# Relative-position attention and a gated MLP on one core: both heads' scores side by side in 64-row tiles, in three products

## Chip, cores, metric

The kernel runs on one core of a Trainium2 chip. The metric is the device time of one execution in microseconds, as the median of several. The engines of the core are PE (matrix products and transposes), DVE, ACT and POOL (element-wise work), and SP, which issues most transfers. PEld in a row of the profile is PE's weight load, which runs beside its matmuls.

## What is computed

```python
scores = (q @ k.T) / sqrt(64)               # batch 8, heads 8, 576 positions, 64 wide
x = log1p(|i - j|) / log1p(max(i, 1))
scores += (relu(x * w1 + b1) @ w2)          # a bias for each head and pair (i, j)
attn = softmax(scores);  y = attn @ v       # y: 4608 tokens x 512
out = ((y @ moe_w1) * (y @ moe_w2)) @ moe_w3 @ moe_w_out
```

All arrays are float32. To keep their precision at the speed of PE's rounded float32 (fp32r), a factor x is split into a rounded part h and the rest l = x - h, and the product is made as a sum of products of such parts.

## The kernel before

**Prologue.** The bias of every head is built with matmuls (L517, tile `bacc`), scaled by ACT (L530, `bev`) and written to memory (`nb_d`). From there it is loaded for each pair of heads as `nb0`, `nb1`, `nb4`, `nb5` and `nbM`.

**Attention.** A unit is one pair of heads of one batch, `units = [(p, b) ...]`: 4 pairs x 8 batches = 32 units. The 576 queries of a head are four tiles of 128 and 64 left over. Tile t = 0 to 7 is head t % 2, queries (t // 2) x 128 on; tile M holds the last 64 queries of both heads in its two halves of partitions. A unit goes through these steps:

- `ldk`, `ldq`, `ldv`: SP loads q, k, v. On the host, q and k were laid out transposed with each head twice, 64 rows above and the same 64 rows below (`_np.concatenate([a, a], axis=2)`), 1152 columns for the two heads.
- `gk`, `gq` (`op_g`): POOL rounds k into K and makes kl = k - K. In Q the upper 64 rows are the rounded part of q and the lower 64 are its rest, so that one product over 128 rows adds both parts.
- `S0` to `S7`, `SM` (`op_S`, L290): PE makes the scores of a tile into `s`, which is two PSUM banks (576 columns as 2 x 288). A tile takes four matmuls, Q with K and with kl for each half of the columns. The pool `ps_s` has two such buffers.
- `T0` to `TM` (`op_T`, L298): DVE adds the bias, scales, and takes the row maximum: `ts`, `mx`. `ts` has three buffers.
- `E0` to `EM` (`op_E`, L321): ACT makes the exponential into `pp` (or `ppM`) and the row sum into `sum`.
- `F0` to `F7`, `FM`, `L0`, `L1`, `N` (`op_F`): PE transposes 128 x 128 blocks into `pst`, four of them in a PSUM bank; `ps_t` has four buffers. N transposes the last columns of tile M and the reciprocals `r`.
- `H...` (`op_H`): ACT or DVE copies `pst` into `pt` and `px`; the table below says which.
- `r`, `rd` (`op_r`): DVE makes the reciprocals of a unit's nine columns of sums (L328, L329); after N and HN they are stored to `r_d` by two transfers.
- `W0`, `W1` (`op_W`, L397): PE multiplies by v, in two tiles of 64 columns of the array at once. `X0`, `X1` copy the result, and `xd` stores it.
- `c0` to `c7`: a piece of the MoE weights is loaded and converted in 24 of the units; c3 to c6 are on DVE.

The order on each engine is written out by hand: `ORDER` gives each step a time within a unit, the next unit's steps follow `PERIOD = 15.82` later, and `drive` issues all steps sorted by time. So an engine runs its instructions in the order of this table, steps of two units mixed, and a step that has to wait holds up what is behind it on its engine:

```python
    "PE": {
        "S0": 0.00, "S1": 1.66, "S2": 2.64, "S3": 4.31, "S4": 5.18, "S5": 8.31, "S6": 8.84, "F0": 9.37, "F1": 12.87,
        "S7": 13.32, "F4": 13.86, "SM": 14.31, "F5": 15.37, "L0": 16.35, "F2": 16.58, "F7": 17.03, "F3": 18.01,
        "FM": 18.99, "L1": 19.44, "F6": 19.67, "N": 20.66, "W0": 21.63, "W1": 25.74,
    },
```

**MoE.** Behind attention the inner weights w3 and w_out are multiplied together (`fold`, L619), and then for each chunk of 512 tokens come `up` (L661) and `down` (L686), three products each. `load_x` reads the attention's result and the reciprocals (`xr`, `rb`), and `split_x` multiplies them.

Of the kernel before, what the change touches and what calls it, by code (L numbers as in the profile page):

```python
# [31 lines left out]
PERIOD = 15.82  # L32
ORDER = {
# [5 lines left out]
    "DVE": {
        "T0": 0.98, "T1": 2.64, "T2": 3.63, "T3": 5.29, "T4": 6.16, "c3": 7.31, "c4": 8.31, "T6": 9.82, "T5": 10.52,  # L40
        "c5": 11.22, "c6": 12.22, "T7": 14.31, "H4": 15.01, "TM": 15.82, "HL0": 17.50, "r": 17.84, "HM": 20.14,
        "HN": 22.68,
    },
# [23 lines left out]
def relpos_attention_moe(  # L67
# [132 lines left out]
    for i in range(2):
        qt = qk.tile([P, 2 * (S + P)], F32R, name=f"Q{i}")
        nc.gpsimd.memset(f(qt[:, S:S + P]), 0.0)
        Q2.append(qt)

    def halves(x):
        return x.rearrange("p (a j) -> p a j", a=2)
# [38 lines left out]
    def op_g(u, n):  # L248

        d = st[u]  # L250
        x = d.pop("r" + n)
        if n == "q":
            Q = Q2[u % 2]
            Qd = halves(Q)[:, :, 0:S]
            x = halves(x)
# [1 line left out]
            nc.gpsimd.tensor_tensor(Qd[hi], x[hi], f(Qd[hi]), op=ALU.subtract)
            d["Q"] = Q
        else:
            K = qk.tile([P, 2 * S], F32R, name="K", bufs=2)  # L260
            kl = qk.tile([P, 2 * S], F32R, name="kl", bufs=2)
            nc.gpsimd.tensor_scalar(K, x, 1.0, 1.0, op0=ALU.mult, op1=ALU.mult)
            nc.gpsimd.tensor_tensor(kl, x, f(K), op=ALU.subtract)
            d.update(K=K, kl=kl)

    def op_S(u, t):
        d = st[u]
        Q, K, kl = d["Q"], d["K"], d["kl"]
        d["s", t] = ps_s.tile([P, 2, 512], F32, name="s")
        for hf in range(2):  # L270
            scores(d["s", t][:, hf, :HS], t, hf, Q, K, kl)

    def scores(s, t, hf, Q, K, kl):
        js = slice(hf * HS, (hf + 1) * HS)
        if t == "M":

            l, m = Q[:, 512:512 + P], Q[:, S + 64:S + 64 + P]
            ops = [(s, l, x[:, js]) for x in (K, kl)]
            if hf == 0:
                ops += [(s, m, x[:, S + 64:S + 64 + HS]) for x in (K, kl)]  # L280
            else:
                ops += [(s[:, 0:512 - HS], m, x[:, S + 64 + HS:2 * S]) for x in (K, kl)]
                ops += [(s[:, 512 - HS:HS], m, x[:, S:S + 64]) for x in (K, kl)]
        else:
            h, i = int(t) % 2, int(t) // 2
            q0 = h * (S + P + 64) + i * P
            l = Q[:, q0:q0 + P]
            ops = [(s, l, x[:, h * S + hf * HS:h * S + (hf + 1) * HS]) for x in (K, kl)]
        for m, (o, l, r) in enumerate(ops):
            nc.tensor.matmul(o, l, r, start=(m == 0), stop=(m == len(ops) - 1))  # L290
# [17 lines left out]
    def op_E(u, t):  # L308
        d = st[u]
        ts, mx = d.pop(("t", t))  # L310
        if "sum" not in d:
# [9 lines left out]
        nc.scalar.activation(pp, ts, AF.Exp, bias=mx, scale=-1.0, accum_out=d["sum"][:, col:col + 1])  # L321

    def op_r(u, n):
        p, b = units[u]
        d = st[u]
        if n == "":
            r = sm.tile([P, 9], F32, name="r")
            nc.vector.tensor_scalar(r, d["sum"], 1e-9, None, op0=ALU.add)  # L328
            nc.vector.reciprocal(r, r)  # L329
            d["r"] = r  # L330
        else:
            rows = r_d[p][:, b * S:(b + 1) * S]
            nc.sync.dma_start(rows[:, 0:512].rearrange("h (i j) -> h i j", j=P), d["rt"][0:8])
            nc.sync.dma_start(rows[:, 512:S].rearrange("(o h) j -> o h j", o=1), d["rt"][8:9])

    def op_F(u, n):
# [1 line left out]
        ps = ps_t.tile([P, 512], F32, name="pst")  # L340
        if n == "N":
            nc.tensor.transpose(ps[lo, 0:P], d["PM"][:, 512:S], ident)
            nc.tensor.transpose(ps[:, P:2 * P], d["PM"][:, S - P:S], ident)
            nc.tensor.transpose(ps[0:9, 2 * P:3 * P], d["r"], ident)
        elif n[0] == "L":
            for c in range(2):
                nc.tensor.transpose(ps[:, c * P:(c + 1) * P], d["P", 2 * int(n[1]) + c][:, 512:512 + P], ident)
        else:
            for c in range(4):
                if n == "M":  # L350
                    x = d["PM"][:, c * P:(c + 1) * P]
                else:
                    c0 = int(n) % 2 * (S + 64) + c * P
                    x = d["P", int(n) // 2][:, c0:c0 + P]
                nc.tensor.transpose(ps[:, c * P:(c + 1) * P], x, ident)  # L355
# [452 lines left out]
```

## Time and profile before

| | |
|---|---|
| device time, median of 3 runs | 1243.39 us (1242.02 to 1244.5) |
| span of the profiled execution | 1241.4 us, 2.0 us below that median |
| attention, first score matmul to last W1 matmul | 63 to 602 us |
| PE, DVE, ACT, POOL busy | 97%, 53%, 49%, 31% of the span |
| granted PE clock | 1.00 from 93 us on |
| DMA | 130.25 MB in 60795 packets |

Each row of the timeline gives start, length, engine, line, operation, output <- inputs, shape and count, and in brackets the idle time ahead of it with what ended it. A matmul's row is longer than its slot, since matmuls are pipelined: its slot is the distance to the next start. PE runs attention with hardly a hole, so its share of 97% says that it is occupied, not that its array is filled.

### The profile page before, as it was taken

The numbers are of one execution on the slowest core, as the hardware profiler recorded it, in microseconds if no ns is written. First come the engines' busy times: TensorE is split into PE (matmuls) and PEld (weight loads), VectorE is DVE, ScalarE is ACT, GpSimd is POOL, SyncE is SP. The second block draws the span as 40 slices with busy tenths as digits, with TensorE's granted clock in tenths as the row PEclk, the third lists the DMA queues.
The fourth block names the chain that finished last, engine by engine and source line by source line (L and its number), as shares of the span: only waits on it lengthen the run. The fifth ranks groups of instructions, "written<-read, shape, count | busy, mean of one in ns | idle before, by whom it ended". The sixth has DMA issues, their size and how long they took to land. (4 is left out here: it accounts for less than half of the span.)

```text
span 1241.4 us, 19015 instructions
## 1 busy us (share of the span) xinstructions
PE 1200.8 (97%) x7136; PEld 956.6 (77%) x7136; DVE 656.6 (53%) x1380; ACT 603.5 (49%) x1303; POOL 390.0 (31%) x260
## 2 busy tenths in 40 slices
PE   7679999999999999999989999999999999999998
PEld 3168887777778887887768788888888888888887
DVE  8647776777677767776999532222222131313111
ACT  7558887888788877888544321212121212121211
POOL 0436664666456655661654300000000000000000
PEclk9879999999999999999999999999999999999999
DMA  7854446444645463431443220212111110200001
GB/s 215 286 172 143 144 149 204 133 142 145 220 133 152 152 219 120 148 94 54 135 132 117 68 74 29 68 34 65 38 51 51 51 51 35 68 34 1 29 7 34
DMA packets 60795, 130.25 MB, mean 105 GB/s; under 512 B 8992, under 2 KB 18592, under 8 KB 60704
## 3 DMA queue, kind: packets, MB, share of 16 engines
q1 hardware_dynamic: 59408, 127.32, 32.7%
q10 hardware_dynamic: 1296, 1.72, 0.5%
q8 instruction: 56, 0.92, 0.3%
q14 instruction: 35, 0.29, 0.1%
HBM read 99.10 MB, written 29.92 MB: 104 GB/s over the span
## 5 line engine op out<-in xcount | busy, mean ns | idle before, releaser
L298 DVE CUSTOM_DVE_ANT_0 ts<-s,nb 128x576 f32<-128x576 f32 x256 | 184.7, 749 | 148.1 <-ACT pt L363 74.1
L661 PE MATMUL up<-xh,wl 128*128 128x512 f32 x576 | 225.4, 391 | 0.1
L669 DVE TENSOR_TENSOR g<-up,a 128x512 f32<-128x512 f32 x72 | 49.7, 690 | 332.2 <-PE up L661 332.2
L661 PE MATMUL up<-xh,wh 128*128 128x512 f32 x576 | 225.3, 391 | 0.0
L661 PE MATMUL up<-xl,wh 128*128 128x512 f32 x576 | 225.3, 391 | 0.0
L290 PE MATMUL s<-K,Q 128*128 128x288 f32 (+2 forms) x672 | 206.0, 326 | 16.2 <-DVE mx L298 7.6
L321 ACT ACTIVATE pp<-ts,mx 128x576 f32<-128x576 f32 x256 | 196.7, 770 | 39.2 <-DVE mx L298 39.1
L290 PE MATMUL s<-kl,Q 128*128 128x288 f32 (+2 forms) x672 | 182.1, 295 | 0.0
L686 PE MATMUL o<-w3s,gh 128*128 128x512 f32 x576 | 177.8, 390 | 0.0
L666 ACT COPY a<-up 128x512 f32<-128x512 f32 x72 | 42.2, 586 | 247.5 <-PE up L661 247.5
L647 POOL TENSOR_SCALAR xh<-xr 128x512 fp32r<-128x512 f32 x36 | 23.9, 664 | 435.7 <-DVE xr L643 432.5
L290 PEld LDWEIGHTS s<-K,Q 128*128 128x128 f32 x672 | 128.3, 191 | 38.2 <-DVE mx L298 18.0
L355 PE MATMUL pst<-ident,pp 128*128 128x128 f32 x1024 | 152.8, 278 | 0.0
L363 ACT ACTIVATE pt<-pst 128x512 f32<-128x512 f32 x224 | 129.5, 594 | 34.2 <-PE pst L355 29.9
L397 PE MATMUL pst<-pt,rv 128*64 128x320 f32 (+1 forms) x1024 | 138.3, 412 | 0.0
L355 PEld LDWEIGHTS pst<-ident,pp 128*128 128x128 f32 x1024 | 118.8, 141 | 15.2 <-DVE wi L148 11.8
L672 ACT ACTIVATE gh<-g 128x512 fp32r<-128x512 f32 x72 | 45.5, 632 | 172.8 <-DVE g L669 172.8
L290 PEld LDWEIGHTS s<-kl,Q 128*128 128x128 f32 x672 | 129.0, 192 | 0.0
L661 PEld LDWEIGHTS up<-xh,wl 128*128 128x128 f32 x576 | 108.2, 188 | 23.9 <-DVE wl L582 0.5
L661 PEld LDWEIGHTS up<-xl,wh 128*128 128x128 f32 x576 | 108.3, 188 | 23.3
L661 PEld LDWEIGHTS up<-xh,wh 128*128 128x128 f32 x576 | 108.3, 188 | 23.2
L686 PEld LDWEIGHTS o<-w3s,gh 128*128 128x128 f32 x576 | 108.2, 188 | 22.8
(85 smaller groups left out, 1720.3 us busy)
## 6 DMA issues: line engine op xcount, KB each, us to landing
rk<-in_k_dram SPq DMA_DIRECT2D x31, 576.0 KB
rq<-in_q_dram SPq DMA_DIRECT2D x31, 576.0 KB
wi<-in_moe_w_dram SPq DMA_DIRECT2D x32, 512.0 KB
nb_d<-bev SPq DMA_DIRECT2D x36, 295.5 KB
rv<-in_v_dram SPq DMA_DIRECT2D x32, 320.0 KB
x_d<-x SPq DMA_DIRECT2D x32, 288.0 KB
xr<-x_d SPq DMA_DIRECT2D x36, 256.0 KB
rb<-r_d SPq DMA_DIRECT2D x72, 128.0 KB
```

What stands on the lines that cost most here:

```text
L290: nc.tensor.matmul(o, l, r, start=(m == 0), stop=(m == len(ops) - 1))
L298: nc.vector.tensor_tensor_reduce(out=halves(ts), in0=d.pop(("s", t))[:, :, :HS], in1=halves(NB[p, t]), op0=ALU.add, op1=ALU.min, scale=-1. ...
L321: nc.scalar.activation(pp, ts, AF.Exp, bias=mx, scale=-1.0, accum_out=d["sum"][:, col:col + 1])
L355: nc.tensor.transpose(ps[:, c * P:(c + 1) * P], x, ident)
L363: nc.scalar.activation(o, x, AF.Copy)
L397: nc.tensor.matmul(acc[rows], x[:, c0:c0 + D], m, start=(c == 0), stop=(c == 4))
L647: nc.gpsimd.tensor_scalar(xh, xr, 1.0, 1.0, op0=ALU.mult, op1=ALU.mult)
L661: nc.tensor.matmul(acc, l[:, cc], r, start=(n == 0), stop=(n == 3 * NC - 1))
L666: nc.scalar.copy(a, ps[0])
L669: nc.vector.tensor_tensor(g, ps[1], a, op=ALU.mult)
L672: nc.scalar.activation(gh, g, AF.Copy)
L686: nc.tensor.matmul(d["o", t], l[:, sl], folded[ft][r], start=(ft == 0 and n == 0), stop=(ft == NF - 1 and n == 2),)
```

## The change

Four things are changed.

1. q is split in both parts like k: `qh`, `ql`, `kh`, `kl`, with head 2p in the upper 64 rows and head 2p + 1 in the lower (576 columns for k, 640 for q, where 512 on holds the last queries of both heads with zeros in the other head's rows). A score is the sum of three products, hh, lh and hl, over 64 rows each. One step makes both heads' tiles, six matmuls for each half of the columns, taking turns between the rows 0 to 63 and 64 to 127, into two buffers of `ps_s`. `S1`, `S3`, `S5`, `S7` leave the table. SM makes its tile over all 128 rows with six matmuls in place of ten.
2. FM transposes the last queries in 64-row tiles, ten transposes into two `pst` buffers, and takes over the part that N had. HM is four copies on DVE in place of one, and HN's two small copies go. `ppM` becomes two fixed tiles `PM2` with 64 zero columns in front.
3. The sums of eight units are kept in one tile of 72 columns; `r`, N, HN and `rd` run only for the last unit of each pair of heads, `rd` then with sixteen transfers.
4. In `ORDER` the T's are spread anew and E2 and E3 change places; nbM is loaded by three transfers.

```diff
@@ ORDER
-        "S0": 0.00, "S1": 1.66, "S2": 2.64, "S3": 4.31, "S4": 5.18, "S5": 8.31, "S6": 8.84, "F0": 9.37, "F1": 12.87,
-        "S7": 13.32, "F4": 13.86, "SM": 14.31, "F5": 15.37, "L0": 16.35, "F2": 16.58, "F7": 17.03, "F3": 18.01,
+        "S0": 0.00, "S2": 2.64, "S4": 5.18, "S6": 8.84, "F0": 9.37, "F1": 12.87, "F4": 13.86, "SM": 14.31, "F5": 15.37, "L0": 16.35, "F2": 16.58, "F7": 17.03, "F3": 18.01,
...
@@ op_g
+        h = qk.tile([P, x.shape[1]], F32R, name=f"{n}h", bufs=2)
+        l = qk.tile([P, x.shape[1]], F32R, name=f"{n}l", bufs=2)
+        nc.gpsimd.tensor_scalar(h, x, 1.0, 1.0, op0=ALU.mult, op1=ALU.mult)
+        nc.gpsimd.tensor_tensor(l, x, f(h), op=ALU.subtract)
+        d[n] = (h, l)
+
+    TERMS = ((0, 0), (1, 0), (0, 1))
@@ op_S
+        i = int(t) // 2
+        ss = [ps_s.tile([P, 2, 512], F32, name="s") for _ in range(2)]
         for hf in range(2):
+            for m, (x, y) in enumerate(TERMS):
+                for s, rows in zip(ss, (lo, hi)):
+                    nc.tensor.matmul(
+                        s[:, hf, :HS], Q[x][rows, i * P:(i + 1) * P], K[y][rows, hf * HS:(hf + 1) * HS],
+                        start=(m == 0), stop=(m == 2),
+                    )
@@ op_r
+        if b < B - 1:
+            return
         if n == "":
+            nc.vector.tensor_scalar(sums[p], sums[p], 1e-9, None, op0=ALU.add)
+            nc.vector.reciprocal(sums[p], sums[p])
+        elif n == "d":
+            for c in range(B):
+                rows, x = r_d[p][:, c * S:(c + 1) * S], rts[p][9 * c:9 * c + 9]
...
@@ op_F
+        if n == "M":
+            d["FM"] = [ps_t.tile([P, 512], F32, name="pst") for _ in range(2)]
+            for c in range(5):
+                for h, (ps, rows) in enumerate(zip(d["FM"], (lo, hi))):
+                    x = PM2[u % 2][rows, c * P + 64:c * P + 64 + (64 if c == 4 else P)]
...
+                    nc.tensor.transpose(ps[0:x.shape[1], c * 64:(c + 1) * 64], x, ident[rows, rows])
@@ op_H
         elif n == "M":
-            move(on, (PT.rearrange("p c (a j) -> p c a j", a=2)[:, :, :, 512:S], ps.rearrange("p (c a j) -> p c a j", c=4, a=2)))
+            for h, (ps, rows) in enumerate(zip(d["FM"], (lo, hi))):
+                move(
+                    on, (PT[:, :, h * S + 512:h * S + S], ps[:, 0:256].rearrange("p (c j) -> p c j", c=4)),
+                    (PX[rows, 512:S], ps[rows, 256:320]),
+                )
```

Where it moves instructions, first on PE, from the F's ahead of the second half of a unit's scores up to W0 (`s` are score buffers, `pst` transposes, `ppM` tile M; the numbers tell buffers apart). Before:

```order
L347 MATMUL pst_2573<-ident_60,pp_2460 128x128
L355 MATMUL pst_2581<-ident_60,pp_2460 128x128 x4
L290 MATMUL s_2587<-K_2297,Q0_119 128x288
L290 MATMUL s_2587<-kl_2298,Q0_119 128x288
L290 MATMUL s_2587<-K_2297,Q0_119 128x288
L290 MATMUL s_2587<-kl_2298,Q0_119 128x288
L342 MATMUL pst_2595<-ident_60,ppM_2528 64x128
L343 MATMUL pst_2595<-ident_60,ppM_2528 128x128
L344 MATMUL pst_2595<-ident_60,r_2547 9x128
L290 MATMUL s_2599<-K_2297,Q0_119 128x288
```

At the same place on PE after:

```order
L338 MATMUL pst_1299<-ident_60,ppM1_857 64x64
L338 MATMUL pst_1300<-ident_60,ppM1_857 128x64
L343 MATMUL pst_1313<-ident_60,pp_1193 128x128
L343 MATMUL pst_1313<-ident_60,pp_1198 128x128
L347 MATMUL pst_1321<-ident_60,pp_1198 128x128 x4
L272 MATMUL s_1339<-kh_1024,qh_1105 128x288
L272 MATMUL s_1340<-kh_1024,qh_1105 128x288
L272 MATMUL s_1339<-kh_1024,ql_1106 128x288
L272 MATMUL s_1340<-kh_1024,ql_1106 128x288
L272 MATMUL s_1339<-kl_1025,qh_1105 128x288
```

S4 stands here now, twelve matmuls that alternate between two score buffers, and behind it comes W0; before, single tiles stood there, with N between them, which now runs once in eight units.

On DVE, from the T of tile 0 on (`ts` <- `s`, with the read of its maximum `mx` as a row of its own; `px` is HL0, `pt` is HM). Before:

```order
L298 ISA ts_3824,mx_3825<-s_3801,nb0_2360 128x576
L298 ISA mx_3825 128x1
L361 COPY px1_860<-pst_3814 128x256
L328 TENSOR_SCALAR r_3841<-sum_3647 128x9
L329 RECIPROCAL r_3841<-r_3841 128x9
L298 ISA ts_3855,mx_3856<-s_3835,nb1_2390 128x576
L298 ISA mx_3856 128x1
L298 ISA ts_3870,mx_3871<-s_3850,nb0_2360 128x576
L298 ISA mx_3871 128x1
L361 COPY pt1_859<-pst_3859 128x8x64
L298 ISA ts_3899,mx_3900<-s_3881,nb1_2390 128x576
```

On DVE after, from the same T to that of tile 3:

```order
L284 ISA ts_3990,mx_3991<-s_3959,nb0_2446 128x576
L284 ISA mx_3991 128x1
L353 COPY px1_863<-pst_3981 128x256
L284 ISA ts_4002,mx_4003<-s_3960,nb1_2467 128x576
L284 ISA mx_4003 128x1
L284 ISA ts_4043,mx_4044<-s_4011,nb0_2446 128x576
L284 ISA mx_4044 128x1
L353 COPY pt1_862<-pst_4026 128x4x64
L353 COPY px1_863<-pst_4026 64x64
L353 COPY pt1_862<-pst_4027 128x4x64
L353 COPY px1_863<-pst_4027 64x64
L284 ISA ts_4062,mx_4063<-s_4012,nb1_2467 128x576
```

The two rows of r are gone from this place, HL0 stands between the T's of one pair as before, and HM between the T's of the next is four copies.

More of the change, by code (lines that the diff above doesn't have):

```diff
@@ L39 @@
     "DVE": {
[L40 to L41 removed]
+        "T0": 0.90, "T1": 1.80, "T2": 3.63, "T3": 4.50, "T4": 6.16, "T5": 7.20, "c3": 8.00, "c4": 9.00, "T6": 9.90,
+        "T7": 10.80, "c5": 11.60, "c6": 12.40, "H4": 15.01, "TM": 15.82, "HL0": 17.50, "r": 17.84, "HM": 20.14,
         "HN": 22.68,
@@ L85, in relpos_attention_moe @@
     nc = tc.nc
-    NPAIR, B, _, S2 = q.shape
-    S, D, H = S2 // 2, P // 2, 2 * NPAIR
+    NPAIR, B, _, S = k.shape
+    D, H = P // 2, 2 * NPAIR
+    SP = q.shape[3]
     HID = w1.shape[1]
@@ L195, in relpos_attention_moe @@
     lo, hi = slice(0, 64), slice(64, 128)
-    NB = {}
+    NB, sums, rts = {}, {}, {}
     st = {u: {"P": [None] * 9} for u in range(NU)}
[L202 to L206, printed above, removed]
     def halves(x):
@@ L238, in load @@
         else:
-            t = raw.tile([P, 2 * S], F32, name=f"r{which}")
+            t = raw.tile([P, src.shape[3]], F32, name=f"r{which}")
         queue = nc.scalar if u == 0 and which != "v" else nc.sync
@@ L266, in op_S @@
+        l = qk.tile([P, x.shape[1]], F32R, name=f"{n}l", bufs=2)
[3 more added lines that the diff above has]
+    TERMS = ((0, 0), (1, 0), (0, 1))
     def op_S(u, t):
         d = st[u]
-        Q, K, kl = d["Q"], d["K"], d["kl"]
-        d["s", t] = ps_s.tile([P, 2, 512], F32, name="s")
-        for hf in range(2):
[L271 to L290, printed above, removed]
@@ new lines, in op_S @@
+        Q, K = d["q"], d["k"]
+        if t == "M":
+            s = d["s", t] = ps_s.tile([P, 2, 512], F32, name="s")
+            for hf in range(2):
+                for m, (x, y) in enumerate(TERMS):
+                    nc.tensor.matmul(
+                        s[:, hf, :HS], Q[x][:, 512:512 + P], K[y][:, hf * HS:(hf + 1) * HS], start=(m == 0), stop=(m == 2),
+                    )
+            return
+        i = int(t) // 2
+        ss = [ps_s.tile([P, 2, 512], F32, name="s") for _ in range(2)]
@@ L292, in op_T @@
+        for hf in range(2):
+            for m, (x, y) in enumerate(TERMS):
+                for s, rows in zip(ss, (lo, hi)):
+                    nc.tensor.matmul(
+                        s[:, hf, :HS], Q[x][rows, i * P:(i + 1) * P], K[y][rows, hf * HS:(hf + 1) * HS],
+                        start=(m == 0), stop=(m == 2),
+                    )
+        d["s", t], d["s", str(int(t) + 1)] = ss
     def op_T(u, t):
@@ L310, in op_E @@
         ts, mx = d.pop(("t", t))
-        if "sum" not in d:
-            d["sum"] = sm.tile([P, 9], F32, name="sum", bufs=3)
+        p, b = units[u]
+        if p not in sums:
+            sums[p] = sm.tile([P, 9 * B], F32, name="sum", bufs=2)
         if t == "M":
-            pp, col = ppool.tile([P, S], F32, name="ppM", bufs=2), 8
-            d["PM"] = pp
+            pp, col = PM2[u % 2][:, P - 64:P - 64 + S], 8
         else:
@@ L320, in op_E @@
             pp, col = d["P", i][:, h * S:(h + 1) * S], i + 4 * h
-        nc.scalar.activation(pp, ts, AF.Exp, bias=mx, scale=-1.0, accum_out=d["sum"][:, col:col + 1])
+        nc.scalar.activation(pp, ts, AF.Exp, bias=mx, scale=-1.0, accum_out=sums[p][:, 9 * b + col:9 * b + col + 1])
     def op_r(u, n):
         p, b = units[u]
-        d = st[u]
+        if b < B - 1:
+            return
         if n == "":
[L327 to L334, printed above, removed]
+            nc.vector.tensor_scalar(sums[p], sums[p], 1e-9, None, op0=ALU.add)
[3 more added lines that the diff above has]
+                rows, x = r_d[p][:, c * S:(c + 1) * S], rts[p][9 * c:9 * c + 9]
+                nc.sync.dma_start(rows[:, 0:512].rearrange("h (i j) -> h i j", j=P), x[0:8])
+                nc.sync.dma_start(rows[:, 512:S].rearrange("(o h) j -> o h j", o=1), x[8:9])
@@ L338, in op_F @@
     def op_F(u, n):
         d = st[u]
-        ps = ps_t.tile([P, 512], F32, name="pst")
[L341 to L345, printed above, removed]
+        p, b = units[u]
+        if n == "N":
+            if b == B - 1:
+                ps = d["FN"] = ps_t.tile([P, 512], F32, name="pst")
+                nc.tensor.transpose(ps[0:9 * B, 0:P], sums[p], ident)
+            return
@@ new lines, in op_F @@
+        if n == "M":
[3 more added lines that the diff above has]
+                    x = PM2[u % 2][rows, c * P + 64:c * P + 64 + (64 if c == 4 else P)]
+                    if h == 1:
+                        x = PM2[u % 2][rows, 0:P] if c == 4 else PM2[u % 2][rows, (c + 1) * P:(c + 2) * P]
+                    nc.tensor.transpose(ps[0:x.shape[1], c * 64:(c + 1) * 64], x, ident[rows, rows])
+            return
@@ L346, in op_F @@
+        ps = ps_t.tile([P, 512], F32, name="pst")
+        if n[0] == "L":
             for c in range(2):
@@ L349, in op_F @@
             for c in range(4):
[L350 to L355, printed above, removed]
+                c0 = int(n) % 2 * (S + 64) + c * P
+                nc.tensor.transpose(ps[:, c * P:(c + 1) * P], d["P", int(n) // 2][:, c0:c0 + P], ident)
         d["F" + n] = ps
@@ L366, in op_H @@
         d = st[u]
+        p, b = units[u]
+        PT, PX = PTX[u % 2]
+        if n == "N":
+            if b == B - 1:
+                rts[p] = sm.tile([9 * B, P], F32, name="rt", bufs=1)
+                move(on, (rts[p], d["FN"][0:9 * B, 0:P]))
+            return
         ps = d["F" + n]
-        PT, PX = PTX[u % 2]
         if n[0] == "L":
@@ L549, in relpos_attention_moe @@
     ps_t = att.enter_context(tc.tile_pool(name="ps_t", bufs=NPS, space=PSUM))
+    PM2 = [ppool.tile([P, P - 64 + S], F32, name=f"ppM{i}") for i in range(2)]
+    for x in PM2:
+        nc.gpsimd.memset(x[:, 0:P - 64], 0.0)
     PTX = [(pt.tile([P, 4, 2 * S], F32, name=f"pt{i}"), pt.tile([P, S], F32, name=f"px{i}")) for i in range(2)]
@@ L774 @@
         a = inputs[n].reshape(-1, pairs, 2, seq, dim)
-        a = _np.stack([a[:, :, 0], _np.roll(a[:, :, 1], seq - 512, axis=2)], axis=2).transpose(1, 0, 4, 2, 3)
-        inputs[n] = _np.concatenate([a, a], axis=2).reshape(pairs, -1, 2 * dim, 2 * seq)
+        x = _np.zeros((pairs, a.shape[0], 2, dim, 640 if n == "q" else seq), a.dtype)
+        a = a.transpose(1, 0, 2, 4, 3)
+        if n == "q":
+            x[:, :, 0, :, :seq] = a[:, :, 0]
+            x[:, :, 1, :, :512], x[:, :, 1, :, seq:] = a[:, :, 1, :, :512], a[:, :, 1, :, 512:]
+        else:
+            x[:, :, 0], x[:, :, 1] = a[:, :, 0], _np.roll(a[:, :, 1], seq - 512, axis=3)
+        inputs[n] = x.reshape(pairs, -1, 2 * dim, x.shape[4])
     a = inputs["v"].reshape(-1, pairs, 2, seq, dim).transpose(1, 0, 2, 3, 4)
```

23 lines of the change are left out of this document (3 added, 20 removed), and 2 rows, old and new, of the table ORDER.

## Prediction

> **What bounds the kernel now.** I read the page first, then the busy times of single units, the waits, and last the timeline of one unit with all engines.
>
> ```profile
> span 1241.4 us, 19015 instructions
> PE 1200.8 (97%) x7136; PEld 956.6 (77%) x7136; DVE 656.6 (53%) x1380; ACT 603.5 (49%) x1303; POOL 390.0 (31%) x260
> 219.91:235.94 16.03, 15.91 (x127) 12.86 (x125) 12.20 (x31) 13.04 (x31) 10.15 (x7) 1.00 0.48 145
> PEld s L290 <- DVE mx L298: 10.6, 28, 0.5
> ```
>
> The third line is one unit of attention, from the last transpose of its N step (L344) to that of the next unit: 16.03 us, in which PE is busy for 15.91, DVE for 12.20 and ACT for 13.04, at a granted clock of 1.00. The fourth, from the waits between 100 and 555 us, says that the scores wait for T only 10.6 us in 28 units, 0.38 us a unit. So attention is a stream of PE work with hardly a hole, 32 units of it; the MoE behind it is PE too, and the change does not touch it. What counts is what a unit costs on PE, and whether PE still never waits.
>
> The durations come from this stretch of the timeline (start, length, engine, line):
>
> ```profile
> 220.42 0.29 PE L290 MATMUL s<-kl,Q 128*128 128x288 f32 x1
> 220.64 1.95 PE L397 MATMUL pst<-pt,rv 128*64 128x256 f32 x16
> 221.55 0.45 DVE L361 COPY px<-pst 64x64 f32<-64x64 f32 x2
> 222.03 0.28 DVE L361 COPY rt<-pst 9x128 f32<-9x128 f32 x1
> 222.95 0.19 PEld L290 LDWEIGHTS s<-K,Q 128*128 128x128 f32 x1 [0.39 <-DVE wmag L134]
> 224.10 0.60 PE L355 MATMUL pst<-ident,pp 128*128 128x128 f32 x4
> 224.41 0.76 DVE L298 CUSTOM_DVE_ANT_0 ts<-s,nb 128x576 f32<-128x576 f32 x1 [1.30 <-PE s L290]
> 225.10 0.75 DVE L298 CUSTOM_DVE_ANT_0 ts<-s,nb 128x576 f32<-128x576 f32 x1
> 227.48 0.66 PE L355 MATMUL pst<-ident,pp 128*128 128x128 f32 x4
> 227.89 0.38 PE L290 MATMUL s<-K,Q 128*128 128x288 f32 x1
> 228.10 0.29 PE L290 MATMUL s<-kl,Q 128*128 128x288 f32 x1
> 228.23 0.29 PE L290 MATMUL s<-K,Q 128*128 128x288 f32 x1
> 228.37 0.29 PE L290 MATMUL s<-kl,Q 128*128 128x288 f32 x1
> 228.50 0.60 PE L355 MATMUL pst<-ident,pp 128*128 128x128 f32 x4
> 228.81 0.76 DVE L298 CUSTOM_DVE_ANT_0 ts<-s,nb 128x576 f32<-128x576 f32 x1 [1.89 <-ACT pt L363]
> ...
> 229.84 0.19 PEld L290 LDWEIGHTS s<-K,Q 128*128 128x128 f32 x1
> 229.95 0.19 PEld L290 LDWEIGHTS s<-kl,Q 128*128 128x128 f32 x1
> ...
> 231.48 2.66 POOL L263 TENSOR_TENSOR kl<-rk,K 128x1152 fp32r<-128x1152 f32 x1
> 232.12 0.42 DVE L361 COPY px<-pst 128x256 f32<-128x256 f32 x1
> 232.45 1.72 DVE L328 TENSOR_SCALAR r<-sum 128x9 f32<-128x9 f32 x1
> 234.34 0.70 DVE L298 CUSTOM_DVE_ANT_0 ts<-s,nb 128x576 f32<-128x576 f32 x1
> 235.09 0.19 PEld L290 LDWEIGHTS s<-K,Q 128*128 128x128 f32 x1 [0.35 <-DVE mx L298]
> 235.33 0.29 PE L290 MATMUL s<-kl,Q 128*128 128x288 f32 x1
> ```
>
> Read off: a score matmul of 288 columns takes a slot of 0.13 us (228.10, 228.23, 228.37); after a wait the first costs 0.11 more, for its weights (235.09 to 235.33 is 0.24), and two weight loads of 128 columns with little between them stand 0.11 apart (229.84, 229.95). T starts 0.44 after the last score matmul starts (228.37, 228.81). Two T's in a row stand 0.69 apart (224.41, 225.10), and PE gets the score buffer back 0.75 after a T starts (234.34, 235.09). A transpose is a slot of 0.11 (the four of 228.50). W0 takes 2.53 from the last score matmul ahead of it to the next score weights (220.42, 222.95). F0 to F1 with W1 between takes 3.38 (224.10, 227.48), an F and the first score matmul 0.41 (227.48, 227.89). On DVE a copy of 128x256 holds its successor 0.33 (232.12, 232.45), two of 64x64 0.48 (221.55, 222.03).
>
> **The change on PE, as work.** The two heads' tiles go as 64-row halves of the array. If both halves run side by side, a pair of tiles costs six slots instead of eight: 4 pairs x 2 x 0.13 = 1.05 us less a unit. The M tile goes from six matmuls of 288 columns, two of 224 and two of 64, eight slots' worth, to six: 0.26 less. The last queries: seven transposes (four FM, three N) become ten in 64-row halves, five slots if side by side: 0.2 less, or 0.3 more if one after the other. No row shows 64-row halves; the nearest are column tiles, which do run side by side, their weights too:
>
> ```profile
> 56.24 1.06 PE L517 MATMUL bacc<-zact,w2b 128*32 128x512 f32 x1
> 56.25 1.06 PE L517 MATMUL bacc<-zdve,w2b 128*32 128x512 f32 x1
> ...
> 13.20 0.11 PEld L517 LDWEIGHTS bacc<-zact,w2b 128*32 128x32 f32 x1
> 13.21 0.12 PEld L517 LDWEIGHTS bacc<-zdve,w2b 128*32 128x32 f32 x3
> ```
>
> Matmuls 1.06 us long start 0.01 apart. I take side by side; the other bound is twelve weight loads at 0.11.
>
> Going in and out of the halves may cost. Into W's column tiles PE takes 0.22 from the last score (220.42 to 220.64) where an F takes 0.13 (228.37 to 228.50): 0.09 more, and a weight load that is not hidden makes it about 0.15. A unit had four such changes (around W0 and W1) and has ten now, six more: 0 to 0.9 us. The Trainium skill says in "TensorEngine Tiling (Array Packing)", Key Properties, that changing the tiling mode drains the engine. The 0.09 agrees with it for column tiles; no run here shows it for 64-row halves. By that rule my final sum would be 5 us higher, since all but one of the new changes fall into waits found below; without it, it stays as it is. Without waits a unit would thus be 16.03 - 0.38 - 1.5 + (0 to 0.9) = 14.1 to 15.0 us.
>
> **The change on PE, as waits.** This term decides. Before, one step S fills one of the two score buffers while T empties the other. Now one step takes both, so its second matmul waits until both T's of the pair before have run, and all behind it on PE waits with it: W0, which needs no scores, stands behind S4. On DVE other work stands between the two T's: HL0 between T0 and T1, and the whole of HM between T2 and T3, while HM itself waits for FM, which PE issues behind S2. HM is now two copies of 128x256 elements and two of 64x64: 2 x 0.33 + 0.48 = 1.14.
>
> The ring, from the moment t at which a pair's second tile may load its weights; its last matmul starts at t + 0.11 + 5 x 0.13 = 0.76, its first T at t + 1.20:
> - S0 to S2: T0 at 1.20, HL0 at 1.89, T1 at 2.22, released 2.97. PE would be there at 0.76 + 0.13 + 14 transposes x 0.11 = 2.4: it waits 0.5.
> - S2 to S4: T2 at 1.20, HM at 1.89 (FM's last transpose starts at 0.89 + 4 x 0.11 = 1.33, its copy can start by 1.65), T3 at 3.03, released 3.78. PE would be there at 0.89 + 5 x 0.11 + 6 x 0.11 = 2.1: it waits 1.7.
> - S4 to S6: 0.76 + 2.53 = 3.29 through W0; T5's buffer is back at 1.20 + 0.69 + 0.75 = 2.64, so no wait.
> - S6 to the next S0: 0.76 + 0.13 to F0, 3.38 to F1, 0.41 + 0.44 for F1 and F4 to SM, whose last of six slots starts 0.21 + 4 x 0.13 = 0.73 later, 0.44 to TM, 0.75 to release: 7.04. S0 needs both buffers and so TM too; PE would be there after F5, 0.6 earlier.
>
> Sum: 2.97 + 3.78 + 3.29 + 7.04 = 17.08 us a unit, against 16.03. On the ring there may lie 0 to 0.16 for leaving the halves at F0, and 0 to 0.30 if FM's ten transposes go one by one: 17.08 to 17.54. I take 17.15, nearest to the column tiles that start together: 1.12 us a unit more, for 30 full units 34 us (bounds 31 to 45).
>
> **Other parts.** Sums and reciprocals once in eight units free DVE of L328, which takes 1.72 us and ends when POOL's L263 does (231.48 + 2.66); it is what delayed the T behind the wait of 0.35 at 235.09. That wait is in the 16.03, and the ring above has no r in it; nothing more is gained. POOL and the loads of q and k halve; POOL is busy 10.15 of 16.03 and off the path. ACT keeps its order but for E2 and E3, which change places: E3 stands behind X0, which waits for W0, and then T6 behind E3, later than the scores allow; but the first on PE to need T6's buffer is SM, 4.2 us behind F0 (3.38 + 0.41 + 0.44).
>
> At the start it does count:
>
> ```profile
> 47.20 4.51 POOL L262 TENSOR_SCALAR K<-rk 128x1152 fp32r<-128x1152 f32 x1 [45.65 <-DMA rk<-in_k_dram]
> 60.55 5.20 POOL L257 TENSOR_TENSOR Q<-rq,Q 64x1152 fp32r<-64x1152 f32 x2
> 63.21 0.61 PE L290 MATMUL s<-K,Q 128*128 128x288 f32 x1 [5.82 <-POOL Q L257]
> 591.99 0.61 SPq L333 DMA_DIRECT2D r_d<-rt  x1
> 598.75 8.16 SPq L123 DMA_DIRECT2D wi<-in_moe_w_dram  x2
> ```
>
> POOL's splits of the first two units run from 47.20 on, the one S0 needs last (the first of the two at 60.55) to 63.15, and PE stands 5.82 us for them with the bias matmuls queued behind. With half the columns they end at least 6 us earlier, so PE could gain 0 to 6; the bias transfers also pace this stretch, and I take 4. At the end, the last pair's sixteen stores of r (0.6 us each on SP's queue) stand ahead of the MoE weights that went out at 598.75: 592 + 9.6 = 601.6, so 0 to 3 us, I take 1. In the other pairs the loads behind them are for a unit later. nbM's extra transfer and the memsets of PM2 are early and single: nothing.
>
> Sum: 1241.4 + 34 - 4 + 1 = 1272 as a span; the median of the runs lies 2.0 above the span shown: **1274 us**, own range 1266 to 1292.
>
> **Rivals.**
> - *Faster: the waits are covered and the work decides.* PE's 14.1 to 15.0 a unit would give 31 x (-1.9 to -1.0) - 4, so 1180 to 1208. It needs the waits (0.5, 1.7 and 0.6, together 2.8) to shrink below 1.0 to 1.9. The break is at the T3 release: it would have to come 1.1 us earlier. For it: PE is the engine that binds now. Against: each wait is a sum of durations that are in the rows, and at 235.09 PE stood still for a T, with nothing queued behind it passing. "TensorEngine Tiling (Array Packing)", Theoretical Speedup, in the Trainium skill promises up to twofold for a contraction of 64 rows or fewer, which is this rival's side; its Gotcha 1, that row tiles write to different banks of PSUM, is the side of the waits. 0.12.
> - *The halves do not run side by side.* With a weight load each at 0.11, a pair's last matmul starts 0.56 later, four times on the ring, and FM adds 0.3: 19.6 a unit, 3.5 x 30 = 107 more, about 1347. For it: twelve loads of 128 columns a pair, and 0.11 is the closest spacing of such loads shown. Against: the column tiles. 0.10.
> - *Gain and waits cancel*, within 0.2%, which is about what a measurement here can tell from no change: 0.05; the ring would have to be 16.0 to 16.2.
>
> My forecast has 0.73. The range 1215 to 1300 holds it and what lies between it and the faster case, leaving out the slow halves and the fast end, under 0.2. Faster 0.13, same 0.05, slower 0.82.
>
> **What the new profile would show.** The unit distance near 17.1; PE waiting for T at the second matmul of S2, S4 and S0, longest at S4 (about 1.7); PE busy per unit below 15.2. Score matmuls of a pair starting in twos 0.13 apart show the halves side by side; twelve starts 0.11 apart, the rival. The first score matmul some 5 us earlier. I am wrong if T3 starts right behind T2, or if S4 starts without a wait.

## The result, and the profile after

The changed kernel takes 1288.15 us (median of 4 runs, 1287.71 to 1289.05), the kernel before in the same session 1242.82 us. The ratio is 1.0362, with a 95% interval from 1.0348 to 1.0377: the change costs 45 us. The forecast was 1274 us (own range 1266 to 1292, stated range 1215 to 1300), so side and cause held and the size fell 14 us short.

From the page of the kernel after, a wait of PE between 130 and 600 us (us in total, times, longest), and the busy times of single units (from the first score matmul of an M tile, L263, to that of the next; the columns are as before: length, busy time of PE, its weight loads, DVE, ACT and POOL, granted clock, DMA share, GB/s):

```profile
span 1286.4 us, 19961 instructions
PE 1205.4 (94%) x7620; PEld 919.7 (71%) x7620; DVE 613.5 (48%) x1328; ACT 593.5 (46%) x1303; POOL 282.0 (22%) x260
PE s L272 <- DVE mx L284: 38.8, 53, 1.5
...
257.82:275.18 17.36, 15.80 (x144) 11.59 (x142) 10.56 (x28) 12.71 (x31) 6.88 (x7) 1.00 0.36 103
...
310.27:329.32 19.05, 17.49 (x143) 12.35 (x142) 10.55 (x28) 12.70 (x31) 6.86 (x7) 0.91 0.33 94
```

PE now has 484 more instructions, is busy for a smaller share of the span (94% against 97%), and stands still for T at line L272. A normal unit takes 17.36 us instead of 16.03 to 16.05. Five of the 31 units take 19.0 us, at a granted clock of 0.91. Two more take 17.72.

One normal unit, with the rows on which the ring rests, to S0's second matmul of the next (start, length, engine, line):

```profile
259.01 0.76 DVE L284 CUSTOM_DVE_ANT_0 ts<-s,nbM 128x576 f32<-128x576 f32 x1 [0.21 <-ACT pp L307]
259.83 0.39 PE L272 MATMUL s<-kh,qh 64*128 64x288 f32 x1 [0.20 <-DVE mx L284]
260.91 0.76 DVE L284 CUSTOM_DVE_ANT_0 ts<-s,nb 128x576 f32<-128x576 f32 x1 [1.13 <-PE s L272]
261.59 0.42 DVE L353 COPY px<-pst 128x256 f32<-128x256 f32 x1
261.93 0.75 DVE L284 CUSTOM_DVE_ANT_0 ts<-s,nb 128x576 f32<-128x576 f32 x1
263.07 0.39 PE L272 MATMUL s<-kl,qh 64*128 64x288 f32 x2
263.20 0.39 PE L272 MATMUL s<-kh,qh 64*128 64x288 f32 x2
263.33 0.39 PE L272 MATMUL s<-kh,ql 64*128 64x288 f32 x2
263.60 0.56 PE L338 MATMUL pst<-ident,ppM 64*128 64x64 f32 x10
263.90 0.76 DVE L284 CUSTOM_DVE_ANT_0 ts<-s,nb 128x576 f32<-128x576 f32 x1 [1.22 <-PE s L272]
264.59 0.42 DVE L353 COPY pt<-pst 128x256 f32<-128x256 f32 x1
265.73 0.76 DVE L284 CUSTOM_DVE_ANT_0 ts<-s,nb 128x576 f32<-128x576 f32 x1
266.64 0.37 PE L272 MATMUL s<-kh,qh 64*128 64x288 f32 x1 [1.35 <-DVE mx L284]
...
267.29 0.38 PE L272 MATMUL s<-kl,qh 64*128 64x288 f32 x2
267.60 1.95 PE L393 MATMUL pst<-pt,rv 128*64 128x256 f32 x16
269.91 0.40 PE L272 MATMUL s<-kh,qh 64*128 64x288 f32 x2
...
270.67 0.29 PE L272 MATMUL s<-kl,qh 64*128 64x288 f32 x2
270.90 0.66 PE L347 MATMUL pst<-ident,pp 128*128 128x128 f32 x4
...
274.33 1.09 PE L347 MATMUL pst<-ident,pp 128*128 128x128 f32 x8
...
277.19 0.39 PE L272 MATMUL s<-kh,qh 64*128 64x288 f32 x1 [0.20 <-DVE mx L284]
```

DVE's row reads as forecast: TM, T0, HL0's copy, T1, T2, HM's copies from 264.59 to T3 at 265.73 (1.14 us, the estimate was 1.14), and 0.91 behind T3's start S4's second matmul, for which PE stood 1.35 us (1.7 forecast: PE came there 0.4 later than put), with W0 queued behind. The score matmuls of a pair start in twos, 0.13 apart: the halves run side by side. FM's ten transposes need no more than 0.56.

The five long units differ from the others at one place, W0 behind the wait at S4:

```profile
247.60 0.37 PE L272 MATMUL s<-kh,qh 64*128 64x288 f32 x1 [1.35 <-DVE mx L284]
248.56 3.59 PE L393 MATMUL pst<-pt,rv 128*64 128x256 f32 x16
...
248.56:252.55 3.99, 3.99 (x21) 2.15 (x20) 2.21 (x6) 0.00 (x0) 0.00 (x0) 0.57 0.00 0
```

The same sixteen matmuls that took 1.95 take 3.59, and the mean clock granted in these 4 us is 0.57: the trace's clock record has 3.41 us of half clock in them. Each such unit loses 1.68 us.

Where the 45.0 us between the two spans lie, by the first score matmul of each unit's M tile: the first of them is 2.8 us earlier than before (80.64 against 83.42), the 31 distances from it to the last sum to 546.96 instead of 498.44 (+48.5, of which 5 x 1.68 = 8.4 are half clock), and the rest behind them is 0.7 shorter (658.8 against 659.5). The first such matmul, before and after:

```profile
83.42 0.59 PE L290 MATMUL s<-K,Q 128*128 128x288 f32 x1
80.64 0.59 PE L263 MATMUL s<-kh,qh 128*128 128x288 f32 x1
```

### The profile page after: what moved, and what is told of

It is laid out like the page before. It is cut to its first block, busy times and chain, and to the rows that moved or that the text cites. A ratio compares the mean times of both kernels' runs of the same rounds, so it can differ in the third digit from the quotient of the medians.

```text
span 1286.4 us, 19961 instructions
## 1 busy us (share of the span) xinstructions
PE 1205.4 (94%) x7620; PEld 919.7 (71%) x7620; DVE 613.5 (48%) x1328; ACT 593.5 (46%) x1303; POOL 282.0 (22%) x260
## 5 line engine op out<-in xcount | busy, mean ns | idle before, releaser
L284 DVE CUSTOM_DVE_ANT_0 ts<-s,nb 128x576 f32<-128x576 f32 x256 | 191.1, 755 | 208.0 <-PE s L272 106.9
L272 PE MATMUL s<-kh,qh 64*128 64x288 f32 x512 | 133.4, 343 | 60.7 <-DVE mx L284 54.8
L355 ACT ACTIVATE pt<-pst 128x512 f32<-128x512 f32 x224 | 126.6, 596 | 61.7 <-PE pst L347 57.4
L272 PEld LDWEIGHTS s<-kh,qh 64*128 64x128 f32 x512 | 76.1, 185 | 107.0 <-issue 58.8
L393 PE MATMUL pst<-pt,rv 128*64 128x320 f32 (+1 forms) x1024 | 145.6, 429 | 0.0
L347 PE MATMUL pst<-ident,pp 128*128 128x128 f32 x1024 | 142.9, 278 | 0.6 <-ACT pp L307 0.6
L347 PEld LDWEIGHTS pst<-ident,pp 128*128 128x128 f32 x1024 | 115.5, 141 | 21.6 <-issue 20.6
L685 PE MATMUL o<-w3s,gl 128*128 128x512 f32 x288 | 112.2, 390 | 0.9 <-DVE gl L674 0.9
L393 PEld LDWEIGHTS pst<-pt,rv 128*64 128x64 f32 x1024 | 70.8, 142 | 52.1 <-issue 10.6
```

The lines of the kernel that those rows point to most:

```text
L272: nc.tensor.matmul(s[:, hf, :HS], Q[x][rows, i * P:(i + 1) * P], K[y][rows, hf * HS:(hf + 1) * HS], start=(m == 0), stop=(m == 2),)
L284: nc.vector.tensor_tensor_reduce(out=halves(ts), in0=d.pop(("s", t))[:, :, :HS], in1=halves(NB[p, t]), op0=ALU.add, op1=ALU.min, scale=-1. ...
L347: nc.tensor.transpose(ps[:, c * P:(c + 1) * P], d["P", int(n) // 2][:, c0:c0 + P], ident)
L355: nc.scalar.activation(o, x, AF.Copy)
L393: nc.tensor.matmul(acc[rows], x[:, c0:c0 + D], m, start=(c == 0), stop=(c == 4))
L685: nc.tensor.matmul(d["o", t], l[:, sl], folded[ft][r], start=(ft == 0 and n == 0), stop=(ft == NF - 1 and n == 2),)
```

## Experiments

The theory: the unit is set by a ring in which a pair's second tile waits for both T's of the pair before, with HL0 and HM on DVE between them; and the half-clock stretches come of PE's stop at S4. The main rival: the extra time is PE's own work in half tiles. Ratios are to the kernel before, timed on the same chip.

**HL0 and HM behind the T's.** DVE's order alone:

```diff
-"TM": 15.82, "HL0": 17.50, "r": 17.84, "HM": 20.14,
+"TM": 15.82, "HL0": 17.70, "r": 17.84, "HM": 20.40,
```

> The changed kernel, with DVE's order alone altered: HL0's copy goes behind T1 instead of between T0 and T1, and HM's four copies behind T3 instead of between T2 and T3. No work is added or removed. Theory A, the ring of waits sets the unit: the S0-S2 leg loses HL0's 0.33 us and the S2-S4 leg HM's 1.14, while W0 behind S4 then waits up to 0.3 for HM; a unit goes from 17.36 to about 16.2 us, PE's wait at S4 from 1.35 to about 0.2, and the half-clock stretches behind that wait go with it: about 1245 us, near the kernel before. Rival B, the extra time is PE's own work and its changes between whole and half tiles, and the waits are only slack: the time stays at 1288 us, the wait at S4 merely turning up at another place. Rival C, HM is now late for W0 by as much as it was early: W0 waits about 1.1 us, a unit stays at 17.3 us, 1285 us.

Measured 1237.02 us, ratio 0.9961 (0.9946 to 0.9976): 51 us less than the changed kernel, and a little faster than the kernel before. A unit's busy times, and the rows of T2, T3, HM's first copy and S4's second matmul:

```profile
256.17:272.12 15.95, 15.53 (x143) 11.41 (x142) 10.47 (x28) 12.71 (x31) 6.89 (x7) 1.00 0.39 112
...
262.06 0.76 DVE L284 CUSTOM_DVE_ANT_0 ts<-s,nb 128x576 f32<-128x576 f32 x1 [1.01 <-PE s L272]
262.74 0.75 DVE L284 CUSTOM_DVE_ANT_0 ts<-s,nb 128x576 f32<-128x576 f32 x1
263.42 0.42 DVE L353 COPY pt<-pst 128x256 f32<-128x256 f32 x1
263.56 0.40 PE L272 MATMUL s<-kh,qh 64*128 64x288 f32 x1 [0.21 <-DVE mx L284]
264.54 1.95 PE L393 MATMUL pst<-pt,rv 128*64 128x256 f32 x16
```

T3 follows T2 at once, the wait at S4 is 0.21, 28 of the 31 units are at 15.93 to 15.96, three at 16.3, and none runs at half clock: 31 x (17.36 - 15.95) + 8.4 = 52. Theory A holds. It had asked for 16.2, since W0 was to wait 0.3 for HM; it starts 0.98 behind S4's second matmul, as in the changed kernel (267.60 - 266.64 = 0.96), so HM costs it nothing. The two legs fall as the ring says: from 2.97 to 2.67 without HL0 between its T's, from 3.82 to 2.70 without HM.

**HM twice.** The opposite direction:

```diff
-on, (PT[...], ps[:, 0:256]...), (PX[rows, 512:S], ps[rows, 256:320]),
+on, *(2 * [(PT[...], ps[:, 0:256]...), (PX[rows, 512:S], ps[rows, 256:320])]),
```

> The changed kernel, with HM's four copies each issued twice in their place between T2 and T3 (the same values are written again). PE has no more work. Theory A (ring of waits): T3, and with it S4's second tile, comes 1.14 us later in each unit: 17.36 to 18.5 us, 32 x 1.14 = 36 us more, about 1325 us; if half-clock stretches follow the longer wait more often, at 1.7 us each, up to 1355. Rival B (PE's own work sets the unit, DVE has slack of some tenths): less than 10 us more, 1288 to 1298 us.

Measured 1360.41 us, ratio 1.0951 (1.0934 to 1.0967). Two units, and S4 and W0 in one:

```profile
262.26:282.47 20.21, 17.45 (x144) 12.24 (x142) 11.67 (x32) 12.76 (x31) 6.88 (x7) 0.92 0.30 89
282.47:301.05 18.58, 15.82 (x144) 11.60 (x142) 11.67 (x32) 12.71 (x31) 6.87 (x7) 1.00 0.35 97
...
252.04 0.37 PE L272 MATMUL s<-kh,qh 64*128 64x288 f32 x1 [2.54 <-DVE mx L284]
252.99 3.33 PE L393 MATMUL pst<-pt,rv 128*64 128x256 f32 x16
```

Units at full clock take 18.58, 1.2 more, as the ring says. But PE's wait is now 2.54 us, and 26 of the 31 units have W0 at half clock, against 5 of 31 with 1.35: 1288 + 31 x 1.2 + 21 x 1.68 = 1360. Here 36 us of late copies cost 72.

**Useless work in the wait.** F6's four transposes, just ahead of S4 on PE, three times over:

```diff
-for c in range(4):
+for c in 3 * list(range(4)) if n == "6" else range(4):
```

> The changed kernel, with the four transposes of F6 issued three times over (the same values into the same tile): 8 more transposes of 0.11 us, 0.87 us of useless PE work a unit, in the place where PE now waits 1.35 us for T3. Theory A (the ring sets the unit, and the half-clock stretches behind S4 come of PE standing idle there): all units take 17.36 us, the five units in thirty of 19.0 us disappear, the mean clock rises to 1.00, and the time falls by about 8 us to 1280 although work is added. Rival B (the ring sets the unit, but the half-clock stretches do not depend on that idle time): 1288 us, with some units of 19 us left. Rival C (PE's work sets the unit): 32 x 0.87 = 28 us more, 1316 us.

Measured 1280.37 us, ratio 1.0312 (1.0295 to 1.0330), 8 us less than the changed kernel, with 256 more matmuls:

```profile
287.38:304.74 17.36, 16.67 (x152) 12.47 (x150) 10.55 (x28) 12.83 (x31) 6.86 (x7) 1.00 0.36 104
...
261.12 0.37 PE L272 MATMUL s<-kh,qh 64*128 64x288 f32 x1 [0.47 <-DVE mx L284]
```

PE works 0.87 us more a unit and the unit is still 17.36: the ring sets it, not PE's work. The wait is 0.47 instead of 1.35, and no unit is at 19. Theory A, to the microsecond. That the half clock comes of PE's standing still at S4 is shown by this and the run before; why with 1.35 us it strikes one unit in six is open in part. The traces' clock records show that its place in time matters. In a run's attention each half-clock stretch lasts 3.41 us, and each starts a whole multiple of 3.41 us behind the one before, as if the clock were set on a fixed beat (inferred from these starts). In the changed kernel the five stops before half clock lay wholly between two beats and began 0.62 to 1.38 us behind one; five others that began there were spared, and so were the 18 full stops that began elsewhere. With HM twice there are 28 stops of 2.54 to 2.56: the four that were spared were cut by a beat into pieces of at most 1.57, and each of the 24 others had a piece of 1.74 or more.

The Trainium skill, in "TensorE: Matmul & The Clock Gate", A second HAM failure mode: psum-queue depth-cycling, tells of a kernel whose PE idles briefly between groups of matmuls and so falls in and out of half clock; the trace agrees, with five half-clock stretches behind stops of 1.35 us. The same page of the Trainium skill, in HAM oscillation — how this bites in real kernels, has the rule that no gap of PE be above some 3.4 us; that does not cover what is seen here: 1.35 us was enough at times, 2.54 mostly.

**The halves in turn.** All matmuls of a pair's first tile, then of its second:

```diff
-for hf in range(2):
-    for m, (x, y) in enumerate(TERMS):
-        for s, rows in zip(ss, (lo, hi)):
+for s, rows in zip(ss, (lo, hi)):
+    for hf in range(2):
+        for m, (x, y) in enumerate(TERMS):
```

> The changed kernel, with the loops over the halves turned round: all six matmuls of a pair's first tile, then all six of its second, so that nothing in a pair can run side by side; same number of matmuls, same results. Theory A (side by side saves PE six slots of 0.13 us a pair, but the second tile's scores now start at once when only its own buffer is free): S0-S2 about 3.3 us (PE's work), S2-S4 about 3.6 (T3 behind HM as now), S4-S6 about 4.2, S6-S0 about 7.3, in sum 18.4 against 17.36; the half-clock stretches go, as the wait at S4 falls to about 0.5: 1288 + 32 - 8 = 1312 us, bounds 1300 and 1325. Rival B (the waits hide what PE saves, so turning the loops costs nothing): 1280 to 1290 us. Rival C (64-row loads are not hidden when they follow each other in one half): a slot of 0.18 to 0.24 us instead of 0.13, 2 to 5 us a unit, 1350 us and more.

Measured 1288.17 us, ratio 1.0372 (1.0356 to 1.0387): the same as the changed kernel. That is the time of rival B, but two things offset each other in it. One unit:

```profile
257.84:275.37 17.53, 17.11 (x143) 13.20 (x142) 10.64 (x28) 12.83 (x31) 6.88 (x7) 1.00 0.35 103
```

A normal unit is 0.17 longer, 5 us in 31, and no unit behind the first has half clock any more, 8.4 less; the difference of 3 us is not quite reached. My 1312 was wrong, because it took the halves to run strictly one behind the other. The trace shows a pair's last score matmul starting 1.15 us after the first (269.73, 270.88), against 0.11 + 5 x 0.13 = 0.76 in alternation and 0.11 + 11 x 0.13 = 1.54 in strict turn. A kernel held by the ring cannot tell what side by side is worth; for that it was run again where PE binds (below).

**Sums and reciprocals alone**, in the kernel before:

```diff
-r = sm.tile([P, 9], F32, name="r")
-nc.vector.tensor_scalar(r, d["sum"], 1e-9, None, op0=ALU.add)
-nc.vector.reciprocal(r, r)
+if b < B - 1:
+    return
+nc.vector.tensor_scalar(sums[p], sums[p], 1e-9, None, op0=ALU.add)
+nc.vector.reciprocal(sums[p], sums[p])
```

> The kernel before, with one part of the change alone: the sums and reciprocals of a group of eight units together (r, its transpose and its copy once in eight units). Theory A (the 0.38 us a unit that PE waited for T in the kernel before comes of r, whose 1.72 us on DVE delay the next T): the wait goes, 0.3 to 0.38 us in 28 units, 9 to 11 us: 1231 to 1233 us, and no r row of 1.7 us but four. Rival B (the T would be late anyway, or PE's stream fills the gap elsewhere): within 2 us of the kernel before, 1240 to 1243 us.

Measured 1229.44 us, ratio 0.9901 (0.9886 to 0.9916). One unit of it:

```profile
262.02:277.59 15.57, 15.57 (x126) 12.76 (x125) 10.86 (x27) 12.95 (x32) 10.17 (x7) 1.00 0.51 152
```

PE is busy in all of the 15.57 us; the unit is 0.46 to 0.48 shorter, the wait of 0.38 and one transpose slot of 0.11. The last unit of each group takes 0.85 more, for eight units' sums at once (16.42, three times). Theory A holds: this part of the change is worth 12 us by itself; in the changed kernel, where the ring sets the unit, it does not show.

**A better order.** From the rows above, four moves in the changed kernel: SM directly behind W1, the transposes that fill the waits spread behind S0 and S2 (F5 and F3 move), TM ahead of H4, HL0 and HM late.

```diff
-"F1": 12.87, "F4": 13.86, "SM": 14.31, "F5": 15.37, ... "F3": 18.01,
+"SM": 12.50, "F1": 12.87, "F4": 13.86, "F5": 15.95, ... "F3": 18.60,
-"H4": 15.01, "TM": 15.82, "HL0": 17.50, "r": 17.84, "HM": 20.14,
+"TM": 15.01, "H4": 15.40, "HL0": 17.70, "r": 17.84, "HM": 20.40,
```

> The changed kernel with the same instructions in another order on two engines. PE: SM directly behind W1 and ahead of F1 and F4 (so that TM is done early and S0 need not wait for it), F5, F2, F7 and F3 spread between S0 and S4. DVE: TM ahead of H4, HL0 behind T1, HM behind T3. Theory A (the ring of waits sets the unit; its legs can be shortened by order alone): S0-S2 about 2.5, S2-S4 about 2.6, S4-S6 about 3.6, S6-S0 about 6.6, in sum 15.3 us, and 14.6 to 15.8 with what PE's own work without waits allows: about 1220 us, with bounds of 1200 and 1240, faster than both. Rival B (PE's own work and mode changes set the unit): 1288 us, no gain. Rival C (F1 and F4 behind SM come late for ACT, and W0 for HM: new waits of about a microsecond): 1250 to 1288 us.

Measured 1249.34 us, ratio 1.0064 (1.0049 to 1.0079): outside theory A's bounds of 1200 and 1240, a miss. A unit, T3, and S4's second matmul:

```profile
259.85:276.15 16.30, 15.73 (x143) 11.40 (x141) 10.64 (x29) 12.70 (x32) 6.88 (x6) 1.00 0.38 110
...
267.62 0.76 DVE L284 CUSTOM_DVE_ANT_0 ts<-s,nb 128x576 f32<-128x576 f32 x1 [1.09 <-ACT pp L307]
268.44 0.40 PE L272 MATMUL s<-kh,qh 64*128 64x288 f32 x1 [0.57 <-DVE mx L284]
```

T3 stands 1.09 us not for scores but for ACT (pp): T's result has three buffers (NTS), and the exponential that reads the oldest has not run. With the score buffers free earlier, another buffer sets the wait. Hence the next two kernels, each with one thing more:

```diff
 # as the order above, and:
-NPP, NTS, NPS = 6, 3, 4
+NPP, NTS, NPS = 6, 4, 4
 # as "HL0 and HM behind the T's", and:
-"F1": 12.87, "F4": 13.86, "SM": 14.31, / "H4": 15.01, "TM": 15.82,
+"F1": 12.87, "SM": 13.40, "F4": 14.31, / "TM": 15.01, "H4": 15.40,
```

> The reordered kernel of the last set (SM ahead of F1 and F4, fillers spread between S0 and S4, TM ahead of H4, HL0 and HM behind the T's), with four buffers instead of three for T's result. Its trace showed 16.30 us a unit, of which S2-S4 took 3.89, because T3 stood 1.09 us for a buffer that ACT's exponential still read. Theory A (that buffer is the wait): T3 starts 0.3 us behind T2's end, S2-S4 falls to about 2.9 (PE's own work there), a unit to 15.3 to 15.5 us: 1216 to 1224 us. Rival B (ACT is late as such, the fourth buffer only moves the wait to F3 or W0 who need ACT's results): 16.0 to 16.3 us a unit, 1240 to 1249 us.

> The kernel with HL0 and HM behind the T's (first set, 15.95 us a unit), with one thing more: on PE the M tile's scores SM go between F1 and F4 instead of behind both, and on DVE TM goes ahead of H4. Theory A (the last wait of size on the ring is S0's second buffer, which TM gives back 0.3 us late): TM is 0.4 us earlier, S6-S0 falls from 7.28 to about 6.95, a unit to 15.6 us: 1237 - 10 = 1227 us. Rival B (PE's work binds at 15.95 already): 1235 to 1238 us. Rival C (H4, now behind TM and 0.8 us later, holds up T0 or the transposes' buffers): 1245 us.

Measured 1219.03 us, ratio 0.9813 (0.9797 to 0.9829), and 1223.03 us, ratio 0.9847 (0.9832 to 0.9862). The first, with the two last T's of its S2-S4 leg, then a unit of the second:

```profile
264.40:279.74 15.34, 15.34 (x143) 11.21 (x141) 10.38 (x28) 12.73 (x32) 6.87 (x7) 1.00 0.38 117
...
270.30 0.76 DVE L284 CUSTOM_DVE_ANT_0 ts<-s,nb 128x576 f32<-128x576 f32 x1 [1.01 <-PE s L272]
270.98 0.75 DVE L284 CUSTOM_DVE_ANT_0 ts<-s,nb 128x576 f32<-128x576 f32 x1
```

```profile
268.12:283.62 15.50, 15.29 (x144) 11.38 (x141) 10.38 (x29) 12.72 (x31) 6.88 (x6) 1.00 0.39 117
```

Both go as theory A asked, the second 4 us below its 1227. In the first, T3 follows T2 at once; at 15.34 us PE is busy all the time, and PE's own work binds again. This is the fastest kernel of the study, 22.6 us under the kernel before in the same session and 69 under the changed one, with every instruction of the change in it.

**Four buffers in the second of them too:**

> The kernel with HL0 and HM behind the T's and SM between F1 and F4 (15.50 us a unit, 1223 us), with four buffers for T's result. Theory A (what is left there is the ring, and T6 and T7 waiting for ACT set it in part, by TM and S0's second buffer): 0.1 to 0.2 us a unit, 1217 to 1220 us. Rival B (T6 and T7 have slack; the rest of the waits come of T0 to T3, which do not wait for these buffers): 1222 to 1224 us.

Measured 1223.18 us, ratio 0.9852 (0.9838 to 0.9867): no gain, as rival B said. Here the fourth buffer helped only where a T on the ring stood for ACT.

**The halves in turn, where PE binds.** The edit of the loops, in the fastest kernel:

> The fastest kernel so far (reordered, four buffers for T's result, 15.34 us a unit, PE with hardly a wait) with the loops over the halves turned round: a pair's first tile, then its second. In the first such run the ring of waits hid what this costs; its trace showed a pair's last score matmul starting 1.15 us behind its first, against 0.77 with the halves in alternation, so even in turn the halves overlapped in part. Theory A (where PE binds, side by side is worth these slots): 4 x 0.38 = 1.5 us a unit, 15.34 to 16.9, 1219 + 47 = 1266 us. Rival B (the halves in turn do not overlap once PE is dense): 4 x 0.78 = 3.1 us a unit, 1316 us. Rival C (waits still set the unit here too): no more than 10 us, 1219 to 1229.

Measured 1259.46 us, ratio 1.0138 (1.0121 to 1.0155). A unit, and one pair (S6) with the transposes behind it:

```profile
263.15:279.82 16.67, 16.67 (x142) 12.54 (x141) 10.38 (x28) 12.84 (x32) 6.87 (x7) 1.00 0.35 108
...
258.37 0.39 PE L272 MATMUL s<-kh,qh 64*128 64x288 f32 x1
...
258.73 0.29 PE L272 MATMUL s<-kl,qh 64*128 64x288 f32 x1
258.74 0.41 PE L272 MATMUL s<-kh,qh 64*128 64x288 f32 x2
...
259.51 0.29 PE L272 MATMUL s<-kl,qh 64*128 64x288 f32 x1
259.72 0.66 PE L347 MATMUL pst<-ident,pp 128*128 128x128 f32 x4
```

A unit is 1.33 longer, and 31 x 1.33 = 41 us agree with the 40 measured: theory A, a little below its 1.5 a unit. The alternation of the halves in the loops is worth that much where PE binds, and nothing measurable in the changed kernel.

## Why the prediction was right, and where it was off

- *Waits decide, not work*: shown from both sides. HL0's and HM's copies moved on DVE take 51 us away with PE's work untouched; 0.87 us a unit of added PE work inside the wait costs nothing.
- *The ring's terms.* From one release of a pair's second score buffer to the next, by the starts of the second tile's weight loads in the unit shown (259.83, 262.80, 266.61, 269.91, 277.19): S0 to S2 2.97 (forecast 2.97), S2 to S4 3.81 (3.78), S4 to S6 3.30 (3.29), S6 to S0 7.28 (7.04). Sum 17.36 against 17.08, and 17.15 taken. That the first two are right so closely is luck, as two terms offset each other: T starts 0.32 to 0.34 behind a pair's last score matmul, not 0.44, and the buffer is back 0.87 to 0.88 behind T's start, not 0.75. The last leg is short by 0.24: from S6's last matmul (270.67) to F0 0.23 pass instead of 0.13, for which I had granted 0 to 0.16 and taken 0.07; from F0 to F1 3.43 instead of 3.38; from TM's start to the release 0.82 instead of 0.75. Over what was taken, the unit is 0.21 longer, 0.21 x 31 = 6.5 us of the miss.
- *The half clock* was no term of the sum: 8.4 us. With the 6.5 above that is 14.9, and the units took 14.5 more than forecast (48.5 - 34); start and end together came out 0.5 lower than put. That it struck only five units, and so left the time inside the range, is luck too.
- *PE's work without waits, 14.1 to 15.0*: too low. With nothing to wait for, the fastest kernel's unit is 15.34, and the kernel before with the sums alone is 15.57. So the halves, FM and the M tile save PE only 0.23 us a unit, not the 1.5 of the slots. Six slots of a pair are 0.78, but from a pair's first matmul to the transposes behind it 0.99 pass in the fastest kernel (259.98 to 260.97). By difference, the entries and exits, put at 0 to 0.9 in all, took about 1.3. Single starts show some 0.9 of that: a pair begins 0.20 behind the transpose ahead of it, and its next two matmuls start 0.24 later, where a whole tile of the other kernel has 0.03 and 0.21; the transpose behind a pair comes 0.22 after its last matmul instead of 0.13. That is 0.2 going in and 0.1 going out, three times a unit each. Next to W nothing changes: 0.22 into it and 0.31 out of it in both kernels. So the faster rival's 1180 to 1208 was out of reach even with its waits gone; its place, the T3 release, was rightly named.
- *PE busy below 15.2 a unit*: wrong, 15.80, for the same reason: most of it is there in the 15.34 as well.
- *The first scores 5 us earlier*: they start 9.6 us earlier, at 53.62 instead of 63.21, but between 65 and 75 us PE is then busy for only 2.81 of 10, with DMA at 0.94 of its time: as feared, the bias transfers pace that stretch (T waits for the loads of `nb`, 4.7 us at the longest), and 2.8 us are left at the first M tile (4 forecast). The stretch behind the last M tile is 0.7 shorter, where 1 more was forecast.

The row of the first scores and the busy times of the ten microseconds behind them, in the kernel after:

```profile
53.62 0.61 PE L272 MATMUL s<-kh,qh 64*128 64x288 f32 x2 [5.74 <-POOL qh L249]
...
65.00:75.00 10.00, 2.81 (x20) 1.70 (x16) 2.54 (x7) 3.65 (x10) 0.23 (x2) 0.64 0.94 244
```

## What to carry to other kernels

When a step starts to take all buffers of a pool at once, its start waits for the last release, so whatever stands on the releasing engine between two releases, however small, lies on the path: move it behind them before judging the step. Count a step's way round the buffers as a sum of durations; if it exceeds the engine's work, faster work buys nothing, and when one wait is removed the trace names the next buffer (here T's result). Packing halves of the array pays in slots and costs at each entry and exit, so few long stretches in one mode should be worth more than many short ones, which no run here has tried.
